# A token-mixing MLP after linear attention on one core: two weight sums of the second product made ahead in device memory, five wide products, and an order written by hand

## The chip, the cores and the metric

The kernel runs on one core of one Trainium2 chip. The metric is the device time of one execution in microseconds (us), the median of several runs. A core has five engines with a queue of instructions each: TensorE (PE, matmuls), VectorE (DVE), ScalarE (ACT), GpSimd (POOL) and SyncE (SP, which here only issues transfers). An engine takes its instructions in order; waits between engines go by semaphores.

## The reference, cut to what matters

```python
x = A_x                                                   # 2048 tokens x 512 channels
h = x + attention(layernorm(x), wqkv, w_phi, wo)          # 32 heads, linear attention with softmax features
g = layernorm(layernorm(h))
u = gelu(einsum("bsd,sf->bdf", g, w1) + b1)               # w1: 2048 x 1792, mixes tokens
y = einsum("bdf,fs->bds", u, w2) + b2                     # w2: 1792 x 2048
out = h + transpose(y)                                    # 2048 x 512
```

All data are float32. The change concerns the last product, with w2, and what is prepared for it.

## The kernel before, in words

Large matmuls are made in three parts. A float32 operand is split into a rounded part "hi" and a remainder "lo" (`split`, lines 55 to 58: ACT copies to hi, another engine subtracts), and hi x hi + hi x lo + lo x hi are accumulated in PSUM.

The program has three stretches. First come the weights of attention, K, V and their sums (to about 121 us of the profile), then the queries, the attention output and the second layer norm, tile by tile (`for it in range(NT + 3)`, line 643, to about 280 us). `fills(it)` puts matmuls of the first MLP product between them. Its weights w1 come by `stream` (line 604): SP loads a block of two row tiles by 256 columns, ACT splits it (L610), `flush` lets DVE make the remainder (L602). `wf` has four buffers of each, and a block serves twelve matmuls.

Second, the rest of the first product (line 751, to about 386 us): seven pairs p of column blocks, each accumulated over 16 row tiles into PSUM `PU`, followed by GELU on ACT (L726). `operands_u(p)` makes the seven right-hand operands of p from its four quarters: for p = 0 and 1 POOL makes the sums (L733 to L736) and ACT and DVE split them into `un`; for the others DVE makes them, into `uf`.

Third, the second product. It is done as seven products of sums instead of eight products of blocks (a Strassen-Winograd scheme), for each pair `sp` of the 16 row blocks of the output (eight pairs) and each p (seven): 56 `STEPS`. Each of the seven products of a step is three matmuls of 256 columns (line 787), accumulated over p into halves of four PSUM banks `bank`; each pair takes the four banks that the pair before did not use. The left-hand operands are sums of four blocks of w2. `stream_w2` (line 767) handles a group of two steps: SP loads 2 x 256 KB into `wraw` (three buffers), DVE makes four sums (L777 to L780), ACT splits 128x1792 elements into `whi` (two buffers, L57), and DVE makes the remainder `wlo` (two buffers, L58). There are 28 groups. After the seventh step of a pair the banks are drained: ACT copies a half bank (L820), DVE does five operations (L821 to L825), and POOL issues two transfers that add the result to `out` in device memory (L827), where h was stored before. The last pair is drained to `hb`, which has h loaded ahead, by ten DVE operations (L836 to L846) and three stores.

In this stretch the order on each engine is chosen by a scheduler of the framework. In parts of the earlier stretches it is written out (`manual_schedule`): there an engine gets its instructions in the order of the program text.

Of the kernel before, what the change touches and what calls it, by code (L numbers as in the profile page):

```python
# [21 lines left out]
NF = F // P  # L22
NG = 8
# [10 lines left out]
def block_kernel(ctx: ExitStack, tc: tile.TileContext, x, xT, wT, phic, wo, w1, b1, w2, b2,  # L34
# [3 lines left out]
    cst = ctx.enter_context(tc.tile_pool(name="cst", bufs=1))  # L38
    big = ctx.enter_context(tc.tile_pool(name="big", bufs=NT + 2))
# [15 lines left out]
    def split(hi, lo, src, lo_engine):  # L55

        nc.scalar.activation(hi, src, AF.Copy)  # L57
        lo_engine.tensor_sub(lo, src, hi)  # L58
# [507 lines left out]
    def s_x(t):  # L566
        HT[t] = ak.tile([P, D], F32, name="h", bufs=4)
        nc.sync.dma_start(HT[t], x[t * P:(t + 1) * P, :])
# [19 lines left out]
    def s_hn(t):  # L588
        hn = ak.tile([P, D], F32, name="hn")
        nc.scalar.activation(hn, HT[t], AF.Identity, scale=r2[:, t:t + 1], bias=VE[t][:, 1:2])  # L590
        HN[t] = big.tile([P, 2, D], F32R, name="hs", tag="big")
        split(HN[t][:, 0], HN[t][:, 1], hn, nc.gpsimd)

    w1v = w1.rearrange("(k p) f -> p k f", p=P)
    w2v = w2.rearrange("(k p) s -> p k s", p=P)
# [8 lines left out]
    def stream(src, k0, n, c0, w):  # L604
# [4 lines left out]
        nc.sync.dma_start(raw, src[:, k0:k0 + n, c0:c0 + w])  # L609
# [4 lines left out]
    PU, WI, LO = {}, {}, []  # L614
# [28 lines left out]
    for it in range(NT + 3):  # L643
# [47 lines left out]
        if it >= 3 and even:  # L691
            s_hn(it - 3)
        for p in range(2):
# [15 lines left out]

    NP = NF // 2  # L710
    HD = D // 2
# [38 lines left out]

    for p in range(NP):
        while FN[p] < NT:
            fill(p, ps_b)
# [10 lines left out]
    GRP = 2  # L764
    AW = {}

    def stream_w2(n):
        steps = STEPS[n:n + GRP]
        raw = ws.tile([P, GRP, 7, P], F32, name="wraw", bufs=3)
        wh_ = ws.tile([P, GRP, 7, P], F32R, name="whi")  # L770
        wl_ = ws.tile([P, GRP, 7, P], F32R, name="wlo")
        for i, (sp, p) in enumerate(steps):
            nc.sync.dma_start(raw[:, i, 0:4].rearrange("p (k i) s -> p k (i s)", k=2),
                              w2v[:, 2 * p:2 * p + 2, sp * 2 * P:(sp + 1) * 2 * P])
            AW[sp, p] = wh_[:, i], wl_[:, i]
        with tc.issue_after(LO[-18]):
            nc.vector.tensor_add(raw[:, :, 4], raw[:, :, 0], raw[:, :, 2])  # L777
            nc.vector.tensor_sub(raw[:, :, 0], raw[:, :, 1], raw[:, :, 0])
            nc.vector.tensor_sub(raw[:, :, 5], raw[:, :, 4], raw[:, :, 1])
            nc.vector.tensor_sub(raw[:, :, 6], raw[:, :, 3], raw[:, :, 5])  # L780
        split(wh_, wl_, raw, nc.vector)


    PROD = ((1, 1, 0, 0, True), (2, 6, 2, 1, True), (3, 3, 3, 1, True), (4, 4, 2, 0, False), (0, 0, 1, 0, True),
            (5, 5, 0, 1, False), (6, 2, 3, 0, False))

    def product(o, a, b, start, stop):
        for i, (x, y) in enumerate(((0, 0), (0, 1), (1, 0))):
            nc.tensor.matmul(o, a[x], b[:, y], start=start and i == 0, stop=stop and i == 2, skip_group_check=True)  # L789

    def products(sp, ps, order):
        for a, b, bk, half, opens in order:
            for p in ps:
                wh_, wl_ = AW[sp, p]
                product(bank[bk][:, half], (wh_[:, a], wl_[:, a]), UB[p, b], p == 0 and opens, p == NP - 1)
# [3 lines left out]

    for n, (sp, p) in enumerate(STEPS):  # L800
        t = 2 * sp
        last = t + 2 == NT
        if n % GRP == 0:
            stream_w2(n)
        if p == 0:
            pools = [ps_f, ps_f, ps_q, ps_q] if sp % 2 else [ps_b] * 4
            bank = [pool.tile([P, 2, HD], F32, name="py", tag="pu") for pool in pools]
        if p < NP - 1 - last:
            products(sp, [p], PROD)
# [3 lines left out]
        by_bank = sorted(PROD, key=lambda m: m[2:4])  # L813
# [3 lines left out]
        if not last:  # L817
            products(sp, [p], by_bank)
            ot = uo.tile([P, 2, 2, HD], F32, name="ot", bufs=1)
            nc.scalar.activation(e[:, 1], bank[0][:, 0], AF.Copy)  # L820
            nc.vector.tensor_add(u2, bank[0][:, 1], e[:, 1])  # L821
            nc.vector.tensor_add(u3, bank[1][:, 0], u2)
            nc.vector.tensor_add(e[:, 0], bank[2][:, 0], u2)
            for i, add in enumerate((u3.unsqueeze(1).to_broadcast([P, 2, HD]), e)):
                nc.vector.scalar_tensor_tensor(ot[:, i], bank[2 + i], b2s[:, t + i:t + i + 1], add,  # L825
                                               op0=ALU.add, op1=ALU.add)
                nc.gpsimd.dma_start(out[(t + i) * P:(t + i + 1) * P, :], flat(ot[:, i]), accum_op=ALU.add)  # L827
# [6 lines left out]
        products(sp, [p - 1, p], by_bank)  # L834
        nc.scalar.activation(e[:, 1], bank[0][:, 0], AF.Copy)
        nc.vector.tensor_add(hb[1][:, 1], bank[0][:, 0], hb[1][:, 1])  # L836
        nc.vector.tensor_add(u2, bank[0][:, 1], e[:, 1])
        nc.vector.tensor_add(hb[1][:, 0], u2, hb[1][:, 0])
        nc.vector.tensor_add(u3, bank[1][:, 0], u2)
        nc.vector.tensor_add(hb[0], hb[0], u3.unsqueeze(1).to_broadcast([P, 2, HD]))  # L840
        nc.vector.tensor_add(hb[0][:, 0], bank[2][:, 0], hb[0][:, 0])
        nc.vector.tensor_add(hb[1][:, 0], bank[2][:, 0], hb[1][:, 0])
        nc.vector.tensor_add(hb[0][:, 1], bank[2][:, 1], hb[0][:, 1])
        nc.sync.dma_start(out[t * P:(t + 1) * P, :], flat(hb[0]))
        for k, q in ((0, nc.scalar), (1, nc.sync)):
            nc.vector.tensor_add(hb[1][:, k], bank[3][:, k], hb[1][:, k])  # L846
            q.dma_start(out[(t + 1) * P:NT * P, k * HD:(k + 1) * HD], hb[1][:, k])
# [14 lines left out]

# [32 lines left out]
```

## Time and profile before

| what | us |
|---|---|
| median of 3 runs | 534.54 (534.31 to 534.79) |
| span of the profiled execution | 532.6 |
| PE busy / DVE busy / ACT busy / POOL busy | 520.8 / 384.4 / 271.9 / 234.8 |
| chain that ended last: second product's matmuls | 26% of the span |
| first product's rest, 280 to 386: PE busy | 106.00 |
| second product, 386.0 to 524.2: PE / DVE / ACT busy | 138.20 / 106.83 / 50.02 |

The span is the time from the first to the last instruction of the one execution that was profiled. The page shows busy time by engine, the chain of work that ended last (followed back from the last instruction) and groups of equal instructions; a group's row ends with the idle time of the engine ahead of it and with what ended that. "windows" gives busy time in stretches of the span, "waits" who waited for whom, "timeline" the instructions in order of time. An instruction's reported duration overlaps a little with the start of the next, so the pace of an engine is read from the distance of starts.

### The profile page before, as it was taken

Reading aid. Unit: us, or ns where it says so; the run is one execution under the profiler, and the core shown is the slowest. Engines: PE = TensorE matmul, PEld = TensorE weight load, DVE = VectorE, ACT = ScalarE, POOL = GpSimd, SP = SyncE. Lnnn points to the kernel's source line nnn. Section 1 sums busy time; section 2 is a strip of 40 time slices with the busy share of each in tenths; the row PEclk is TensorE's granted clock in tenths of the full one; section 3 lists DMA queues with packets and bytes.
Section 4 is the critical chain, followed back from the end, with each engine's and each line's share of the span. In section 5 each row is a group of like instructions: output and inputs, shape, how many; then the busy total and the mean of one; then the engine's idle time right before and its main releaser. Section 6 shows DMA issues by size and latency. Waiting matters only on the chain.

```text
span 532.6 us, 9386 instructions
## 1 busy us (share of the span) xinstructions
PE 520.8 (98%) x3616; PEld 448.7 (84%) x3616; DVE 384.4 (72%) x680; ACT 271.9 (51%) x460; POOL 234.8 (44%) x190
## 2 busy tenths in 40 slices
PE   8999999999999989999999999999999999999995
PEld 7888888886877767777788888888899999999995
DVE  6993999877699989875325524835668877887784
ACT  6998844424336776557746423525444243343340
POOL 2589699877889988887325000000001101100110
PEclk9999999999999999999999999999999999999999
DMA  8633310020502233334255333542014556535631
GB/s 309 206 110 118 99 22 21 1 72 9 160 0 79 82 101 116 104 116 136 85 176 159 98 100 98 159 117 82 20 41 107 143 148 153 123 120 136 143 75 46
DMA packets 45486, 55.81 MB, mean 105 GB/s; under 512 B 3969, under 2 KB 33025, under 8 KB 45441
## 3 DMA queue, kind: packets, MB, share of 16 engines
q1 hardware_dynamic: 43136, 51.38, 30.7%
q0 software_dynamic: 2016, 3.67, 5.5%
q8 instruction: 28, 0.46, 0.4%
q10 hardware_dynamic: 288, 0.17, 0.1%
q14 instruction: 18, 0.14, 0.1%
HBM read 46.81 MB, written 8.39 MB: 104 GB/s over the span
## 4 chain that ended last, share of the span: by engine, by line
PE 83%; POOL 9%; DVE 3%; ACT 2%; issue 1%; DVEq 0%; POOLq 0%; ACTq 0%
PE py L789 26%; PE pu L62 11%; PE pu L63 11%; PE pu L64 11%; POOL ez L442 4%; POOL eq L460 3%; PE pv L63 2%; PE pv L64 2%; PE pv L62 2%; PE pk_ps L62 2%; PE pk_ps L63 2%; PE pk_ps L64 2%; POOL hs L58 2%; PE po L62 1%; PE kvp L207 1%; PE po L63 1%
## 5 line engine op out<-in xcount | busy, mean ns | idle before, releaser
L827 POOL DMA_DIRECT2D out<-ot x14 | 12.5, 1001 | 212.2 <-DVE ot L825 212.2
L789 PE MATMUL py<-uf,whi 128*128 128x256 f32 x560 | 96.2, 283 | 0.0
L63 PE MATMUL pu<-hs,whi 128*128 128x512 f32 x224 | 87.6, 391 | 1.8 <-POOL hs L58 1.8
L602 DVE TENSOR_TENSOR wlo<-wraw,whi 128x512 fp32r<-128x512 f32 x56 | 50.3, 903 | 51.8 <-ACT whi L610 50.7
L57 ACT ACTIVATE whi<-wraw 128x1792 fp32r<-128x1792 f32 x28 | 47.7, 1705 | 77.9 <-PE py L789 73.8
L62 PE MATMUL pu<-hs,whi 128*128 128x512 f32 x224 | 87.4, 395 | 0.0
L64 PE MATMUL pu<-hs,wlo 128*128 128x512 f32 x224 | 87.2, 390 | 0.0
L789 PEld LDWEIGHTS py<-uf,whi 128*128 128x128 f32 x560 | 83.3, 192 | 0.0
L789 PE MATMUL py<-uf,wlo 128*128 128x256 f32 x280 | 69.9, 283 | 0.0
L58 DVE TENSOR_TENSOR wlo<-wraw,whi 128x1792 fp32r<-128x1792 f32 x28 | 56.6, 2022 | 15.4 <-ACT whi L57 15.4
L610 ACT ACTIVATE whi<-wraw 128x512 fp32r<-128x512 f32 x56 | 35.0, 627 | 47.0 <-PE pu L63 44.8
L63 PEld LDWEIGHTS pu<-hs,whi 128*128 128x128 f32 x224 | 42.1, 188 | 11.0 <-POOL hs L58 2.8
L62 PEld LDWEIGHTS pu<-hs,whi 128*128 128x128 f32 x224 | 42.0, 188 | 10.9 <-issue 2.5
L64 PEld LDWEIGHTS pu<-hs,wlo 128*128 128x128 f32 x224 | 42.0, 188 | 9.1 <-DVE wlo L602 0.4
L789 PEld LDWEIGHTS py<-uf,wlo 128*128 128x128 f32 x280 | 49.7, 192 | 0.0
L442 POOL TENSOR_TENSOR ez<-eq,zB 128x1024 f32<-128x1024 f32 x16 | 40.9, 2559 | 2.5 <-ACT zB L488 2.5
L789 PE MATMUL py<-un,whi 128*128 128x256 f32 x224 | 38.4, 283 | 0.0
L195 POOL TENSOR_TENSOR pk<-pk,sk 128x1024 f32<-128x1024 f32 x16 | 31.0, 1941 | 9.8 <-DVE sk L194 9.0
L460 POOL TENSOR_TENSOR eq<-eq,w 128x1024 f32<-128x1024 f32 x16 | 32.0, 1997 | 4.0 <-DVE w L457 4.0
L789 PEld LDWEIGHTS py<-un,whi 128*128 128x128 f32 x224 | 33.2, 192 | 0.1
L199 POOL TENSOR_TENSOR zacc<-zacc,pk 128x1024 f32<-128x1024 f32 x13 | 31.3, 2405 | 0.6
L58 POOL TENSOR_TENSOR hs<-hn,hs 128x512 fp32r<-128x512 f32 x16 | 21.4, 1340 | 17.5 <-ACT hs L57 15.6
(165 smaller groups left out, 1176.5 us busy)
## 6 DMA issues: line engine op xcount, KB each, us to landing
wraw<-in_w SPq DMA_DIRECT2D x112, 256.0 KB, 2.9
xraw<-in_xT SPq DMA_DIRECT2D x16, 256.0 KB, 3.1
xh<-in_x SPq DMA_DIRECT2D x16, 256.0 KB, 2.6
h<-in_x SPq DMA_DIRECT2D x16, 256.0 KB, 2.7
out<-h SPq DMA_DIRECT2D x16, 256.0 KB, 3.0
out<-ot POOLq DMA_DIRECT2D x14, 256.0 KB, 4.8
wraw<-in_wT SPq DMA_DIRECT2D x12, 256.0 KB, 5.0
wo<-in_wo SPq DMA_DIRECT2D x4, 256.0 KB, 3.6
```

What stands on the lines that cost most here:

```text
L57: nc.scalar.activation(hi, src, AF.Copy)
L58: lo_engine.tensor_sub(lo, src, hi)
L62: nc.tensor.matmul(o, ah, bh, start=first, stop=False)
L63: nc.tensor.matmul(o, ah, bl, start=False, stop=False)
L64: nc.tensor.matmul(o, al, bh, start=False, stop=last)
L195: nc.gpsimd.tensor_mul(heads(PK[t]), heads(PK[t]), sk.unsqueeze(2).to_broadcast([P, 2 * H, DH]))
L199: nc.gpsimd.tensor_add(zacc, zacc, PK[t])
L442: nc.gpsimd.tensor_mul(EZ[t], EQ[t], zB)
L460: nc.gpsimd.tensor_mul(heads(EQ[t]), heads(EQ[t]), W[t].rearrange("p g c h -> p (g c h)").unsqueeze(2).to_broadcast([P, 2 * H, DH]))
L602: LO.append(nc.vector.tensor_sub(wl_, raw, wh_).ins)
L610: nc.scalar.activation(wh_, raw, AF.Copy)
L789: nc.tensor.matmul(o, a[x], b[:, y], start=start and i == 0, stop=stop and i == 2, skip_group_check=True)
```

## The change

1. **Layout.** The host lays w2 out by groups: `w2[g]` holds four blocks of 128 x 256 (two steps side by side), g = 0 to 27. Only the arrangement changes, no arithmetic is done there.
2. **Sums in device memory.** A scratch tensor `w2s` in device memory gets block 0 of each group twice by plain transfers from SP (`copies_w2`, two groups of both copies in 2 x 256 KB per iteration of the attention loop, iterations 1 to 14), and then blocks 1 and 2 of the group are added to the copies by accumulating transfers from POOL (`adds_w2`, eight of them for four or three groups each, queued after the last POOL operation of the second layer norm). So A+B and A+C of the blocks A, B, C, D come from memory.
3. **A group's preparation.** SP loads the two sums and B, C, D (256 + 384 KB). DVE makes two more sums (L805, L806), ACT splits (L807, `whi` now with three buffers), DVE makes the remainder (L816).
4. **Wide products.** Five of the seven products get a whole bank: one matmul of lhs hi with 512 columns (rhs hi and lo side by side, so hi x hi falls in one half of the bank, hi x lo in the other), and one of lhs lo x rhs hi with 256 columns into the first half. The drain adds the halves. Two products stay as three matmuls of 256, as the last product of the last pair does. A pair takes six banks of eight in turn.
5. **Drain.** Twelve DVE operations of 256 columns instead of five (two of them of 512); fourteen instead of ten for the last pair. The sixth and seventh step of every pair are done together, product by product.
6. **Order.** From the second product on, `manual_schedule` holds for PE, DVE and ACT.
7. The space kept for descriptors of POOL's transfers is 8192 bytes per partition.

Cut to its core:

```diff
+        if 0 < it < 15:
+            with tc.issue_after(HT["ins"]):
+                copies_w2(2 * it - 2, 2 * it)
...
+    def copies_w2(g0, g1):
+        first = w2[g0:g1, 0].rearrange("g p f -> g (p f)")
+        for k in range(2):
+            nc.sync.dma_start(rows(w2s[g0:g1, k].rearrange("g p f -> g (p f)"), 32), rows(first, 32))
+    def adds_w2(g0, g1):
+        nc.gpsimd.dma_start(rows(w2s[g0:g1].rearrange("g k p f -> g (k p f)"), 64),
+                            rows(w2[g0:g1, 1:3].rearrange("g k p f -> g (k p f)"), 64), accum_op=ALU.add)
...
     for p in range(NP):
+        if p < 4:
+            for g in range(7 * p, 7 * p + 7, 4):
+                with tc.issue_after(HN["ins"]):
+                    adds_w2(g, min(g + 4, 7 * p + 7))
         while FN[p] < NT:
             fill(p, ps_b)
...
+    def load_w2(g):
+        RAW[g] = ws.tile([P, 7, GRP * P], F32, name="wraw", bufs=3)
+        nc.sync.dma_start(RAW[g][:, 0:2], w2s[g].rearrange("k p f -> p k f"))
+        nc.sync.dma_start(RAW[g][:, 2:5], w2[g, 1:4].rearrange("k p f -> p k f"))
+    def sums_w2():
+        ...
+        load_w2(g)
+        raw = RAW[g]
+        WH[g] = ws.tile([P, 7, GRP * P], F32R, name="whi", bufs=3)
+        nc.vector.tensor_add(raw[:, 5], raw[:, 1], raw[:, 2])
+        nc.vector.tensor_add(raw[:, 6], raw[:, 4], raw[:, 5])
+        nc.scalar.activation(WH[g], raw, AF.Copy)
+    def lo_w2():
+        ...
+        wl_ = ws.tile([P, 7, GRP * P], F32R, name="wlo", bufs=2)
+        nc.vector.tensor_sub(wl_, RAW[g], WH[g])
...
+    with tc.issue_after(LO[-18]), tc.issue_after(LD[-20]):
+        sums_w2()
+        lo_w2()
+        sums_w2()
...
+        if half is None:
+            nc.tensor.matmul(o, a[0], b, start=start, stop=stop, skip_group_check=True)
+            nc.tensor.matmul(o[:, 0], a[1], b[:, 0], start=False, stop=stop, skip_group_check=True)
+            return
...
+    ctx.enter_context(tc.manual_schedule(engines={ET.PE, ET.DVE, ET.Activation}))
...
+        if n % GRP == 0 and p < NP - 1:
+            lo_w2()
+            sums_w2()
...
+            nc.scalar.activation(e[:, 1], bank[0][:, 0], AF.Copy)
...
+            out_block(0, 0, bank[2][:, 1], u3)
+            out_block(0, 1, bank[3][:, 0], u3, bank[3][:, 1])
+            nc.gpsimd.dma_start(out[t * P:(t + 1) * P, :], flat(ot[:, 0]), accum_op=ALU.add)
+            if n % GRP == 0:
+                lo_w2()
+            out_block(1, 0, bank[4][:, 0], e[:, 0], bank[4][:, 1])
+            out_block(1, 1, bank[5][:, 0], e[:, 1], bank[5][:, 1])
+            nc.gpsimd.dma_start(out[(t + 1) * P:(t + 2) * P, :], flat(ot[:, 1]), accum_op=ALU.add)
+            if n % GRP == 0:
+                sums_w2()
```

More of the change, by code (lines that the diff above doesn't have):

```diff
@@ L763, in block_kernel @@
     STEPS = [(sp, p) for sp in range(NT // 2) for p in range(NP)]
[L764 to L781, printed above, removed]
@@ L802, in block_kernel @@
         last = t + 2 == NT
-        if n % GRP == 0:
-            stream_w2(n)
+        if n % GRP == 0 and p < NP - 1:
+            lo_w2()
+            sums_w2()
         if p == 0:
[L806 to L809, printed above, removed]
+            bank = []
+            for _ in range(6):
+                pool = (ps_f, ps_q, ps_b, ps_b)[n_bank % 8 // 2]
+                bank.append(pool.tile([P, 2, HD], F32, name="py", tag="pu"))
+                n_bank += 1
+        order = LAST if last else PROD
+        if p < NP - 2:
+            products(sp, [p], order)
             continue
```

99 lines of the change are left out of this document (63 added, 36 removed).

## The prediction

> **What bounds the kernel now.** I read the page's busy row and chain first, then the windows, the chain in order of time, and the waits of the last stage.
>
> ```profile
> span 532.6 us, 9386 instructions
> PE 520.8 (98%) x3616; PEld 448.7 (84%) x3616; DVE 384.4 (72%) x680; ACT 271.9 (51%) x460; POOL 234.8 (44%) x190
> ...
> PE 83%; POOL 9%; DVE 3%; ACT 2%; issue 1%; DVEq 0%; POOLq 0%; ACTq 0%
> ```
> ```profile
> 280.00:386.00 106.00, 106.00 (x470) 87.80 (x469) 55.76 (x107) 46.35 (x84) 7.97 (x8) 1.00 0.35 104
> 386.00:524.20 138.20, 138.20 (x1154) 138.20 (x1154) 106.83 (x166) 50.02 (x42) 12.48 (x14) 1.00 0.48 115
> ```
> ```profile
> 277.65 0.91 PE pu L62 x4
> 385.99 138.25 PE py L789 x1152
> 524.26 0.39 ACT e L835
> 524.68 0.42 DVE hb L836
> ...
> 528.48 0.33 DVE hb L846
> ```
>
> TensorE (PE) bounds the kernel, and in the last two stages without a gap: 106.00 busy of 106.00 us in the first MLP product, 138.20 of 138.20 in the second. In a window row the numbers after the length are PE, PEld, DVE, ACT, POOL. The chain gives the pace: 138.25 / 1152 = 120.0 ns for a matmul of 256 columns, and about 0.91 / 4 = 227 ns for one of 512. The second product has 1176 of them: 141.1 us. The granted clock is 1.00. So PE is worth something per instruction, but only as long as VectorE (DVE, 106.83 us in that window) and ScalarE (ACT, 50.02) deliver the split weights in time. How far they are from the path today:
>
> ```profile
> ACT whi L57 <- PE py L789: 73.8, 25, 3.3
> DVE wlo L58 <- ACT whi L57: 14.9, 12, 3.0
> ```
> ACT waits 73.8 us in 25 waits for PE to give a whi buffer back: the split runs one whole group ahead and stands idle, because the sums of the next group were already made while it waited.
>
> **The change, part 1: PE.** Five of the seven products of a step become one matmul of 512 columns and one of 256 instead of three of 256: 227 + 120 = 347 ns instead of 360. A step is then 5 x 347 + 2 x 360 = 2455 ns instead of 2520, a group (two steps) 4.91 us. Over 49 steps, and 7 with four wide products: 49 x 65 + 7 x 52 = 3.5 us. PE alone would need 137.6 us.
>
> **Part 2: the order written out for DVE and ACT.** The sums drop from four to two a group, but the manual order puts them in a closed loop. At each even step the program says: remainder of group g (wlo, after L816), sums of g+1 (L805, L806), split of g+1 on ACT (L807); the remainder of g+1 comes at the next even step, first on DVE. The split needs its sums, the sums stand behind the previous remainder in DVE's queue, and the next remainder needs the split. Nothing in this circle overlaps with itself. Its pieces, from the timeline of before:
>
> ```profile
> 441.04 0.42 DVE L779 TENSOR_TENSOR wraw<-wraw 128x256 f32<-128x256 f32 x1
> 441.37 0.42 DVE L822 TENSOR_TENSOR u<-py,u 128x256 f32<-128x256 f32 x1
> ...
> 441.71 0.41 DVE L823 TENSOR_TENSOR e<-py,u 128x256 f32<-128x256 f32 x1
> ...
> 443.69 2.01 DVE L58 TENSOR_TENSOR wlo<-wraw,whi 128x1792 fp32r<-128x1792 f32 x1
> 445.62 0.42 DVE L777 TENSOR_TENSOR wraw<-wraw 128x256 f32<-128x256 f32 x1
> 446.07 0.42 DVE L778 TENSOR_TENSOR wraw<-wraw 128x256 f32<-128x256 f32 x1
> ...
> 446.43 1.71 ACT L57 ACTIVATE whi<-wraw 128x1792 fp32r<-128x1792 f32 x1 [3.33 <-PE py L789]
> ...
> 448.17 2.03 DVE L58 TENSOR_TENSOR wlo<-wraw,whi 128x1792 fp32r<-128x1792 f32 x1 [0.88 <-ACT whi L57]
> ```
> The remainder gives DVE free after 445.62 - 443.69 = 1.93 us; a sum followed by one that needs it takes 446.07 - 445.62 = 0.45; the second sum ends 0.42 later; ACT takes 1.71; the remainder starts 448.17 - 446.43 - 1.71 = 0.03 after it, and I put 0.05 for the hand-over to ACT. Loop: 1.93 + 0.45 + 0.42 + 0.05 + 1.71 + 0.03 = 4.59 us a group, against 4.91 on PE. That alone would just do.
>
> But the results of each pair of row blocks are drained in the same DVE queue, and ACT's copy of bank 0 stands behind the split of the next group. The drain has twelve DVE instructions of 256 columns (before: five). Six need their predecessor, 0.45 each; six don't, 441.37 - 441.04 = 0.33 each: 4.7 us. ACT's copy puts 0.3 more into the circle:
>
> ```profile
> L820 ACT ACTIVATE e<-py 128x256 f32<-128x256 f32 x7 | 2.7, 385 | 6.0 <-PE py L789 6.0
> ```
> (385 ns, less what overlaps at its ends.) So each of seven drains adds 5.0 us to the circle; where the remainder is put into the middle of the drain (every other pair), the sums still stand behind its last four instructions, so the sum is the same. Two pairs are seven groups: 7 x 4.59 + 2 x 5.0 = 42.1 us on DVE and ACT, and 14 x 2.455 = 34.4 on PE. **The circle is the longer one; PE waits for wlo.** Three whi buffers don't help, because it is the order, not a buffer, that closes it.
>
> Stage: the remainder of group 2 needs the wlo buffer of group 0, 4.9 us in; from there 25 loops to group 27, 25 x 4.59 = 114.8, and 0.3 because the first still goes by PE; 7 x 5.0 = 35.0 of drains; the last remainder 2.1; the last two steps on PE 4.9. Together 162.0 us, against 141.1: **+20.9**. If the hand-overs are 0.08 and 0.05 longer, it is 25 x 0.1 = 2.5 more; if the drain's dependent instructions go at 0.38, 3 less. Range of this term: +18 to +24.
>
> **Part 3: tail.** After the last matmul (its last bank needs one add) DVE's chain is what ends last, now and then. Before, ten adds follow bank 0, from 524.68 to 528.81, 1.7 us after PE's end (385.99 + 141.1 = 527.1). After, bank 0 is ready 4.2 us ahead of the end, and fourteen adds with the same pace end about 2.1 us after it: **+0.4**.
>
> **Part 4: the transfers.** 28 copies of 256 KB, two per iteration, go into SP's queue after the loads of h; 8 accumulating transfers of 1 and 0.75 MB go into POOL's queue, in front of the first operands_u.
>
> ```profile
> q1 hardware_dynamic: 43136, 51.38, 30.7%
> q0 software_dynamic: 2016, 3.67, 5.5%
> ```
> ```profile
> wraw<-in_w SPq DMA_DIRECT2D x112, 256.0 KB, 2.9
> ```
> The copies move 7.3 MB more; at q1's rate (30.7% of 532.6 us for 51.38 MB) that is 23 us of all engines, spread over some 110 us in which the 16 engines are idle two thirds. A w1 block has four buffers of 12 matmuls, 10.9 us, for a landing of 2.9; I cost the copies at nothing, and up to 3 us if a load of h or w1 stands behind two of them. The adds, at q0's rate, are 7.3 / 3.67 x 5.5% x 532.6 = 59 us of all engines, beside a stage whose own share is 0.35 of 106 us: 37 + 59 of 106. Full, but the first w2s block is wanted only some 50 us later. What costs is their issue on POOL:
>
> ```profile
> L827 POOL DMA_DIRECT2D out<-ot x14 | 12.5, 1001 | 212.2 <-DVE ot L825 212.2
> ```
> ```profile
> 273.45 1.30 POOL L58 TENSOR_TENSOR hs<-hn,hs 128x512 fp32r<-128x512 f32 x1 [1.97 <-DMA wraw<-in_w]
> 280.26 0.73 POOL L733 TENSOR_TENSOR tt<-u 128x256 f32<-128x256 f32 x1 [5.51 <-ACT u L726]
> ...
> 289.92 1.68 POOL L736 TENSOR_TENSOR tt<-u,tt 128x256 f32<-128x256 f32 x1
> ```
> ```profile
> 285.16 0.64 ACT L610 ACTIVATE whi<-wraw 128x512 fp32r<-128x512 f32 x1
> ...
> 291.63 0.85 ACT L57 ACTIVATE un<-tt 128x768 fp32r<-128x768 f32 x1 [1.89 <-POOL tt L736]
> ```
> An accumulating transfer of 256 KB in 128 runs occupies POOL 1.0 us. Eight of them cost 8.0 us if the count of transfers sets it, 14.0 if the runs do (256 and 192 instead of 128: 4 x 2.0 + 4 x 1.5), 28 if the bytes do. I take 11, between the first two. POOL is free from 274.75; with the adds it starts operands_u at 274.75 + 11 = 285.8 instead of 280.26, 5.5 late. Behind it in ACT's queue stand un and then w1's splits. The last split ahead of them (285.16) leaves PE some 10.9 us of work, to 296; a little of un's lateness is made up by POOL and ACT closing up. The second un would end at 292.5 + 5.5 = 298.0 and the next split 0.7 later, less some 0.7 closed up: **+2.0** on PE (none at 8, about 5 at 14, about 19 at 28).
>
> The Trainium skill says in "DMA: Bandwidth & Descriptors", section "Anatomy of one DMA", that descriptor generation is small and that many descriptors can be emitted before the incremental cost shows up. By that the issue is 8.0 us, PE loses nothing here and the sum is 2.0 less; no row of this trace has an accumulating transfer of another size.
>
> ACT's order there changes too. In the built order one split of w1 stands behind both GELUs of the pair p = 2 and an uf split, where before three splits stood ahead of them:
>
> ```profile
> 298.31 0.69 ACT L726 ACTIVATE u<-pu,b1s 128x512 f32<-128x512 f32 x1 [1.63 <-PE pu L64]
> 298.90 0.62 ACT L610 ACTIVATE whi<-wraw 128x512 fp32r<-128x512 f32 x1
> 299.42 0.68 ACT L726 ACTIVATE u<-pu,b1s 128x512 f32<-128x512 f32 x1
> ```
> GELU needs PE's last matmul of the pair, and PE's next matmul needs that split: 0.57 + 0.57 + 0.31 + 0.63 and hand-overs of 0.1 = **+2.2** once, which nothing hides.
>
> Sum: 20.9 + 0.4 + 2.0 + 2.2 = +25.5, a span of 558.1. The median stands 534.54 - 532.6 = 1.9 above the profiled span, so 560.0 us.
>
> **Rivals.** *A, faster: PE stays the bound.* If DVE and ACT kept ahead (the splits of two groups in flight, as before), only part 1 and the tail would count: 532.6 - 3.5 + 0.4 + 1.9 = 531.4 us, 533.6 with the ACT order's 2.2. For it speaks that DVE has fewer busy us in sum (28 x 2 sums less, 7 x 7 drain instructions more). Against it: it holds from a loop of (34.4 - 10.0) / 7 = 3.5 us a group, and the remainder and the split alone are 1.93 + 1.71 = 3.64. Chance 0.05, a third of it within 0.2%. By the Trainium skill, "TensorE: Matmul & The Clock Gate", section "Wait — 56ns, not 53.3ns?", a matmul costs its columns at 2.4 GHz and some 2.5 ns, so a wide product would save 2.5 ns and not 13; A would be 2.8 us longer by it. The rows (120.0 and 227 ns) say 13.
>
> *B, much slower: the adds starve w1.* If issue goes by bytes (28 us on POOL) or w1's loads wait behind the adds, the first product loses about 19 us instead of 2: 577 us. The filled engines (0.35 share and 59 us more) speak for it, the 10.9 us of buffered w1 against. Chance 0.10.
>
> *C, the circle is only half closed.* If DVE drains while ACT splits (1.71 us hidden in each drain), the stage is 7 x 1.71 = 12 us shorter: 548 us. ACT's copy behind the split speaks against it in both kinds of pair. Chance 0.08.
>
> Forecast: 0.77. The range 547 to 571 takes in the bounds of the stage (-3, +3), of the issue (-2, +3), of the copies (+3) and C, and leaves out A and most of B. This kernel's measurement tells about 0.2% from no change. Faster 0.04, within 0.2% 0.01, slower 0.95.
>
> **What would show it.** In the profile after: py matmuls of about 137.6 us in all, with some 24 us of idle before them put down to DVE wlo; ACT's split released by DVE wraw instead of PE; DVE wlo released by ACT whi in most of its 28 cases; starts of wlo 4.6 us apart within a pair and about 9.5 us across a drain in every other pair; POOL's eight issues of about 1.4 us between 275 and 290; two gaps of about 2 us on PE near 297 to 305. I am wrong if PE shows no idle in the second product, or if DVE waits for DMA there.

## The result, and the profile after

The changed kernel takes **574.24 us** (572.69 to 575.46), the kernel before 534.48 (534.31 to 534.79) beside it: a ratio of 1.074, 95% interval 1.0718 to 1.0762. The forecast of 560.0 had the direction, and the time lies 3 us above the top of its range.

The profiled execution of the changed kernel, from its page: the span, the busy times, and the shares of PE and of the DMA engines in forty slices.

```profile
span 571.5 us, 8913 instructions
PE 531.5 (93%) x3343; PEld 437.5 (77%) x3343; DVE 384.8 (67%) x677; ACT 271.0 (47%) x460; POOL 240.8 (42%) x198
...
PE   8999999999999899999996899999987987888886
...
DMA  8534200024405555663899775320263653653541
```

PE, 98% busy before, is 93% busy, and its row has two soft places: a digit 6 in the twenty-second slice (300 to 314 us, in the first MLP product), and sevens and eights through the second product. The DMA row has an 8 and two 9s up to the first place (slices 20 to 22, 271 to 314 us). So there are two losses, and the windows give their sizes (length, then PE, PEld, DVE, ACT, POOL busy, granted clock, DMA share, GB/s):

```profile
280.00:398.20 118.20, 109.58 (x472) 88.89 (x471) 51.52 (x93) 48.55 (x85) 9.85 (x12) 0.99 0.65 167
398.20:566.40 168.20, 147.81 (x903) 128.26 (x902) 113.10 (x182) 47.93 (x42) 12.09 (x14) 0.98 0.46 112
307.30:310.60 3.30, 3.30 (x8) 2.62 (x9) 0.60 (x1) 0.00 (x0) 0.00 (x0) 0.50 1.06 225
```

The second product begins at 398.2 instead of 386.0, **12.2 us later**, and lasts 168.2 us instead of before's 141 (its 1176 matmuls at 120.0 ns), **27 longer**; the tail is 0.8 shorter (571.5 - 566.4 = 5.1 against about 5.8). Together 38.6 of the 571.5 - 532.6 = 38.9 us. The last row is one of the stretches of about 3.4 us that follow an idle gap: PE is busy there, but at a granted clock of 0.50.

**The second product.** Who waited for whom from 399 us on:

```profile
ACT whi L807 <- DVE wraw L806: 50.2, 16, 4.7
ACT whi L807 <- issue: 48.7, 6, 8.1
DVE wlo L816 <- ACT whi L807: 32.4, 17, 2.2
...
PE py L832 <- DVE wlo L816: 11.9, 13, 1.4
...
PE py L835 <- DVE e L874: 6.7, 3, 2.4
```

Before, ACT's split waited for PE (73.8 us): it ran ahead. Now it waits for DVE's sums, DVE's remainder waits for ACT's split, and PE waits for the remainder: the closed circle of the forecast. Another 6.7 us PE waits at three drains until DVE has read a bank; there DVE waits for ACT's copy, which stands behind a split (15.1 us in all). (For 48.7 us of ACT's idle time, in six waits, the profile shows no releaser: "issue".) One turn of the circle, in the timelines of DVE and ACT:

```profile
466.80 2.03 DVE L816 TENSOR_TENSOR wlo<-wraw,whi 128x1792 fp32r<-128x1792 f32 x1 [1.90 <-ACT whi L807]
468.74 0.42 DVE L805 TENSOR_TENSOR wraw<-wraw 128x256 f32<-128x256 f32 x1
469.19 0.42 DVE L806 TENSOR_TENSOR wraw<-wraw 128x256 f32<-128x256 f32 x1
471.51 2.03 DVE L816 TENSOR_TENSOR wlo<-wraw,whi 128x1792 fp32r<-128x1792 f32 x1 [1.89 <-ACT whi L807]
```
```profile
469.78 1.70 ACT L807 ACTIVATE whi<-wraw 128x1792 fp32r<-128x1792 f32 x1 [3.01 <-DVE wraw L806]
```

From remainder to remainder it is 471.51 - 466.80 = 4.71 us, in which DVE idles 1.89 and ACT 3.01: each waits while the other works.

**The first product.** ACT splits the blocks of w1 there. Before, from 280 to 386 us, it waited for PE to free a buffer:

```profile
ACT whi L610 <- PE pu L63: 41.1, 23, 2.1
```

Now, from 280 to 399 us and in ACT's timeline:

```profile
ACT whi L614 <- DMA wraw<-in_w: 18.7, 6, 5.2
```
```profile
306.54 0.63 ACT L614 ACTIVATE whi<-wraw 128x512 fp32r<-128x512 f32 x1 [4.20 <-DMA wraw<-in_w]
312.36 0.63 ACT L614 ACTIVATE whi<-wraw 128x512 fp32r<-128x512 f32 x1 [5.18 <-DMA wraw<-in_w]
318.17 0.63 ACT L614 ACTIVATE whi<-wraw 128x512 fp32r<-128x512 f32 x1 [5.18 <-DMA wraw<-in_w]
```

A block comes every 5.8 us, and PE uses one up in 12 matmuls of 227 ns, 2.7 us. The reason is in the transfers: for each queue its packets, MB and share of the 16 engines, and the issues with their time to landing, from 280 to 320 us.

```profile
q0 software_dynamic: 1810, 6.89, 86.2%
q1 hardware_dynamic: 2406, 2.33, 20.0%
...
wraw<-in_w SPq DMA_DIRECT2D x9, 256.0 KB, 17.0
```

The adding transfers (q0) hold the engines, and a load of w1 (q1) takes 17.0 us to land instead of 2.9. The same view from 304 to 316 us, where three blocks run late one behind another:

```profile
q0 software_dynamic: 561, 2.16, 90.1%
q1 hardware_dynamic: 561, 0.54, 16.7%
```

**561 packets of each queue.** By these counts the engines serve the two queues in turn, one packet of each, though one costs much more than the other. By share, 12 us and 16 engines that is 0.901 x 12 x 16 / 561 = 0.308 us for one that adds, 0.167 x 12 x 16 / 561 = 0.057 us for one of a load. A block of w1 is 256 KB in packets of 1 KB, 16 on each engine, so it takes 16 x (0.308 + 0.057) = 5.8 us while adding transfers are queued. That is the distance of the splits above. (The two shares add up to 107%, so the reported times of packets overlap a little. Counted without them: 2.16 MB are 527 packets of 4 KB, and 12 x 16 / 527 = 0.364 us for one of each, again 5.8 us a block.) The Trainium skill has the rule in "DMA: Bandwidth & Descriptors", section "Queues, rings and completion order" (each engine takes turns between queues packet by packet); the trace agrees, and the durations of the packets are the trace's.

### The profile page after: what moved, and what is told of

Its sections match the earlier page's. It is cut to its first block, busy times and chain, and to the rows that moved or that the text cites. A ratio compares the mean times of both kernels' runs of the same rounds, so it can differ in the third digit from the quotient of the medians.

```text
span 571.5 us, 8913 instructions
## 1 busy us (share of the span) xinstructions
PE 531.5 (93%) x3343; PEld 437.5 (77%) x3343; DVE 384.8 (67%) x677; ACT 271.0 (47%) x460; POOL 240.8 (42%) x198
## 5 line engine op out<-in xcount | busy, mean ns | idle before, releaser
L887 POOL DMA_DIRECT2D out<-ot x7 | 6.1, 869 | 232.7 <-DVE ot L883 232.7
L807 ACT ACTIVATE whi<-wraw 128x1792 fp32r<-128x1792 f32 x28 | 47.6, 1701 | 115.1 <-DVE wraw L806 52.0
L67 PE MATMUL pu<-hs,whi 128*128 128x512 f32 x224 | 88.7, 400 | 8.6 <-ACT whi L614 8.6
L68 PE MATMUL pu<-hs,whi 128*128 128x512 f32 x224 | 88.2, 394 | 1.8 <-POOL hs L63 1.8
L816 DVE TENSOR_TENSOR wlo<-wraw,whi 128x1792 fp32r<-128x1792 f32 x28 | 56.6, 2023 | 36.9 <-ACT whi L807 33.9
L831 PE MATMUL py<-uf,whi 128*128 128x512 f32 x195 | 71.1, 398 | 0.0
L832 PE MATMUL py<-uf,wlo 128*128 128x256 f32 x195 | 55.7, 286 | 8.5 <-DVE wlo L816 8.5
L832 PEld LDWEIGHTS py<-uf,wlo 128*128 128x128 f32 x195 | 36.9, 189 | 11.4 <-DVE wlo L816 11.4
L831 PEld LDWEIGHTS py<-uf,whi 128*128 128x128 f32 x195 | 36.8, 189 | 6.9
L831 PE MATMUL py<-un,whi 128*128 128x512 f32 x78 | 31.4, 426 | 1.8 <-DVE ot L881 1.1
L835 PE MATMUL py<-uf,whi 128*128 128x256 f32 x170 | 32.0, 282 | 0.0
```

Of the source, the lines that this page charges most:

```text
L67: nc.tensor.matmul(o, ah, bh, start=first, stop=False)
L68: nc.tensor.matmul(o, ah, bl, start=False, stop=False)
L807: nc.scalar.activation(WH[g], raw, AF.Copy)
L816: nc.vector.tensor_sub(wl_, RAW[g], WH[g])
L831: nc.tensor.matmul(o, a[0], b, start=start, stop=stop, skip_group_check=True)
L832: nc.tensor.matmul(o[:, 0], a[1], b[:, 0], start=False, stop=stop, skip_group_check=True)
```

## The experiments

Each is the changed kernel, or the experiment that is named, with the edit shown. The kernel before was run beside them each time, at 534.41 to 534.85 us.

### e1_swap: the order of sums and remainder

```diff
-            lo_w2()
             sums_w2()
+            lo_w2()
...
             if n % GRP == 0:
+                sums_w2()
                 lo_w2()
             out_block(1, 0, bank[4][:, 0], e[:, 0], bank[4][:, 1])
...
-            if n % GRP == 0:
-                sums_w2()
```

> Only the order of two calls is swapped: at each even step the two sums of group g+2 come ahead of the remainder of g+1 on DVE (in the drain of every other pair both come after the first row block), so ACT's split and DVE's remainder are of different groups and can run side by side. Theory (the circle DVE sums, ACT split, DVE remainder bounds the second product): its 168.5 us fall to about 143, starts of the remainder (wlo) 4.9 us apart like PE's groups, total about 549. Rival 1 (the loads of w2s or their landing bound it): no change, 574. Rival 2 (the wide matmuls are slower than counted): no change beyond 2 us.

Measured: 549.88 us (547.63 to 550.73), ratio 1.0276 (1.025 to 1.0302). The second product takes 146.3 us instead of 168.3; the gaps in the first are as they were. Calling the sums first takes 22 us back, so the circle is the order that was written, not the amount of DVE's work. In the timeline of DVE the sums now stand ahead of the remainder, and while ACT splits what they made, DVE has something to do:

```profile
456.66 0.41 DVE L805 TENSOR_TENSOR wraw<-wraw 128x256 f32<-128x256 f32 x1
457.11 0.42 DVE L806 TENSOR_TENSOR wraw<-wraw 128x256 f32<-128x256 f32 x1
457.45 2.02 DVE L816 TENSOR_TENSOR wlo<-wraw,whi 128x1792 fp32r<-128x1792 f32 x1
```

The remainder starts right behind the sums, with no wait for ACT.

### e2_addsmall: issue without traffic

The eight adding transfers keep their number and their runs, but move 64 of 1024 columns; so 15/16 of the two sums made in memory are left out.

```diff
-        nc.gpsimd.dma_start(rows(w2s[g0:g1]..., 64), rows(w2[g0:g1, 1:3]..., 64), accum_op=ALU.add)
+        nc.gpsimd.dma_start(rows(w2s[g0:g1]..., 64)[:, :, 0:64], rows(w2[g0:g1, 1:3]..., 64)[:, :, 0:64], accum_op=ALU.add)
```

> The eight accumulating transfers keep their count and their runs but move 64 of each 1024 columns, so 15/16 of two sums are left out of the result. Theory (the traffic of the adds starves the loads of w1 between 304 and 319 us): the gaps of 3.1, 1.6 and 3.2 us on PE go, the first product ends 7 to 11 us earlier, total 563 to 567. Rival (the issue of the adds on POOL costs the time): still 574, with the same late operands_u.

Measured: 560.94 us (560.81 to 561.52), ratio 1.0491 (1.0475 to 1.0507). The window of the first product, and POOL's eight issues:

```profile
280.00:385.70 105.70, 105.70 (x468) 87.50 (x467) 52.09 (x93) 47.46 (x85) 9.84 (x11) 1.00 0.45 123
```
```profile
L630 POOL DMA_DIRECT2D w2s<-in_w x8 | 8.4, 2416 | 0.0
```

PE is busy 105.70 of 105.70 us in the first product, and POOL's issue takes 8.4 us just as in the changed kernel. So the 12 us lost there don't come from the issue. The gap that ACT's order makes at 301 us in the changed kernel is gone too; with the smaller transfers the scheduler placed that split between the two GELUs again, so this run takes away both, and the traffic's share is the 12.2 less the 2.1 us of that gap. The second product still takes 168.3 us.

### e3_narrow: three narrow matmuls in place of the wide product

```diff
-            nc.tensor.matmul(o, a[0], b, start=start, stop=stop, skip_group_check=True)
+            nc.tensor.matmul(o[:, 0], a[0], b[:, 0], start=start, stop=stop, skip_group_check=True)
+            nc.tensor.matmul(o[:, 1], a[0], b[:, 1], start=False, stop=stop, skip_group_check=True)
```

> The five wide products go back to three matmuls of 256 columns, with banks, drain and order of the changed kernel. Theory (circle): PE has 27 us idle in the second product and takes the 280 matmuls more out of that; total within 1 us of 574.2. Rival (PE's wide matmuls, seen at 232 to 241 ns, hold the second product): total changes by more than 2 us, up to 3.5 us longer if PE is the bound.

Measured: 574.34 us (573.07 to 574.53), ratio 1.0732 (1.0714 to 1.075), against 574.24 for the changed kernel. Nothing changes: in this kernel what PE does per matmul is worth nothing, because PE isn't the bound.

### e4_spread: later adding transfers

e1_swap, with the adding transfers moved: those for groups 0 to 13 behind the two `operands_u` on POOL, and those for groups 14 to 27 behind the output transfers of the first two row pairs.

```diff
+            for g in range(7 * p, 7 * p + 7, 4):
+                with tc.issue_after(HN["tt"]):
+                    adds_w2(g, min(g + 4, 7 * p + 7))
...
+            if sp < 2:
+                for g in range(7 * sp + 14, 7 * sp + 21, 4):
+                    with tc.issue_after(sent):
+                        adds_w2(g, min(g + 4, 7 * sp + 21))
```

> Swap of e1, and the adds spread: groups 0 to 6 after operands_u(0), 7 to 13 after operands_u(1), the rest on POOL after the output transfers of the first two pairs of the second product. Theory (circle, and traffic of the adds against w1): second product about 143 us, first product 7 to 10 us shorter than in e1, total 536 to 542. Rival (adds hurt wherever they are, now the loads of the second product): the second product has stalls on DMA, total above 546.

Measured: 560.41 us (559.31 to 562.99), ratio 1.0486 (1.0455 to 1.0517). My expectation fell, and the rival that I had named held. The first product is nearly whole again (one gap of 1.82 us at 308.57), but the second takes 166.5 us. Its waits from 388 to 470 us:

```profile
DVE wraw L804 <- DMA wraw<-in_w: 24.3, 2, 12.3
PEld py L831 <- DVE wlo L815: 19.0, 4, 9.8
```

Two bursts of 1.8 MB hold up the loads of w2 by up to 12.3 us, just as the burst in the first product holds up those of w1. So moving a burst elsewhere doesn't cure it; whether spreading does, e9_paced tests.

### e5_pool: the two sums on POOL, nothing in memory

No copies and no adding transfers. POOL makes A+C and A+B from the loaded blocks, and its order is written by hand too; on DVE the order of e8_swap2 (below).

```diff
-        nc.sync.dma_start(RAW[g][:, 0:2], w2s[g].rearrange("k p f -> p k f"))
+        nc.sync.dma_start(raw[:, 0], w2[g, 0])
         nc.sync.dma_start(raw[:, 2:5], w2[g, 1:4].rearrange("k p f -> p k f"))
+        nc.gpsimd.tensor_add(raw[:, 1], raw[:, 0], raw[:, 3])
+        nc.gpsimd.tensor_add(raw[:, 0], raw[:, 0], raw[:, 2])
...
+        if g + 3 < NGR:
+            load_w2(g + 3)
```

> No copies and no adding transfers; the two sums that they made in memory are made by GpSimd, which has nothing but seven pairs of output transfers to issue in the second product, one group of four loads ahead of VectorE's two sums; VectorE's remainders stand ahead of its sums in most steps, behind them where a row pair has just begun draining. If the adding transfers cost the first product 9 us and the circle of VectorE and ScalarE cost the second 27, both are gone: the first product ends as in the kernel before but for the 2.3 us gap of the order of ScalarE, the second takes PE's own time with five wide products, 138 to 142 us instead of 141.0, and the whole is 531 to 538. Rival: GpSimd's sums (0.7 to 1.0 us each at 128x256 by its rows in the first product) make the blocks late, so that the second product stays above 146 us and the whole above 541.

Measured: 542.26 us (542.0 to 543.09), ratio 1.0136 (1.0119 to 1.0153). The first product ends as before, at 385.8 us: without the transfers there is nothing left to explain there. The second takes 149.9 us, so the rival held. Two waits from 395 us to the end, and two groups of DVE:

```profile
POOL wraw L789 <- DMA wraw<-in_w: 101.6, 19, 52.0
ACT whi L804 <- DVE wraw L803: 78.1, 14, 8.2
```
```profile
L803 DVE TENSOR_TENSOR wraw<-wraw 128x256 f32<-128x256 f32 x23 | 13.2, 574 | 0.8
L802 DVE TENSOR_TENSOR wraw<-wraw 128x256 f32<-128x256 f32 x23 | 11.8, 513 | 6.3 <-POOL wraw L789 6.3
```

A block passes through one more engine between its load and the split, with the same three buffers, and a load can start only when the remainder three groups back has been made. DVE's sums also take 574 and 513 ns on average instead of 425 and 420. That is POOL's adds beside them: of the 23 instructions of L803 the 15 that overlap with none take 424 to 427 ns, the 8 that do 843 to 924.

### e6_pool_narrow: e5_pool with narrow products

The edit of e3_narrow in e5_pool.

> As e5_pool, with the five wide products written as three narrow ones again. If PE is the bound there, this costs what a wide product saves, 280 times: 13 ns each by the prediction's working gives +3.6 us against e5_pool, 6 ns by the cadence in the trace of the changed kernel +1.7, 2.5 ns +0.7. If PE is not the bound there, nothing.

Measured: 545.6 us (544.42 to 546.42), ratio 1.0199 (1.018 to 1.0217), 3.3 us above e5_pool. Since e5_pool's PE waits for remainders, that isn't a clean price of the wide product; e10_paced_narrow gives it.

### e7_adds1k: shorter runs

```diff
-    ... rearrange("g k p f -> g (k p f)"), 64) ...
+    ... rearrange("g k p f -> g (k p f)"), 256) ...
```

> The changed kernel with the same bytes added in runs of 1 KB instead of 4 KB. If the long packets are what keeps the loads of w1 waiting (each takes its transfer engine for 333 ns, an ordinary 1 KB packet for about 50), shorter ones let the loads in more often: the first product ends near 387 us instead of 398, and the whole is 562 to 566. If it is the bytes, nothing changes: 573 to 576. If GpSimd's issue follows the number of runs, its eight instructions take over 20 us instead of 8.4 and the traffic is spread over a longer time.

Measured: 577.43 us (577.29 to 577.85), ratio 1.0797 (1.078 to 1.0813). What it should tell is hidden by a new loss. The transfers and the issues, 280 to 320 us, then POOL's and ACT's timelines:

```profile
q0 software_dynamic: 6780, 6.83, 106.5%
...
wraw<-in_w SPq DMA_DIRECT2D x7, 256.0 KB, 7.1
```
```profile
274.76 7.28 POOL L630 DMA_DIRECT2D w2s<-in_w  x4
286.95 1.77 POOL L630 DMA_DIRECT2D w2s<-in_w  x1 [4.91 <-issue]
```
```profile
306.69 1.06 ACT L62 ACTIVATE un<-u 128x1024 fp32r<-128x1024 f32 x1 [19.86 <-POOL u L753]
```

The loads of w1 do land sooner, after 7.1 us instead of 17.0. But an issue now takes 7.28 / 4 = 1.82 us instead of 1.05, the last four are held up, and POOL comes to operands_u only at 304.4 us. ACT's un, ahead of w1's splits in its queue, waits 19.86 us for POOL, and PE has one gap of 13.7 us. This is the first variant of rival B, made by runs and not by bytes. The row of q0 also gives 1.065 x 640 / 6780 = 0.100 us for an adding packet of 1 KB (at most: a share above 100% says that the reported times overlap). By the byte that is dearer than the long ones (0.40 us for 4 KB), but a block of w1 would take only 16 x (0.100 + 0.057) = 2.5 us beside them. e11 and e12 test that with nothing on POOL behind the issue.

### e8_swap2: the order alone, carried through

The transfers of the changed kernel; in the first two steps of a row pair the remainder goes first, then the sums; in the others the sums first; in an even pair's drain both stand behind the first row block.

```diff
-            lo_w2()
-            sums_w2()
+            for make in (lo_w2, sums_w2) if p < 2 else (sums_w2, lo_w2):
+                make()
...
             if n % GRP == 0:
                 lo_w2()
+                sums_w2()
             out_block(1, 0, bank[4][:, 0], e[:, 0], bank[4][:, 1])
...
-            if n % GRP == 0:
-                sums_w2()
```

> The changed kernel with its transfers as they are, and the order of e5_pool on VectorE: remainders ahead of sums in the first two steps of a row pair, sums ahead of remainders in the others, and in an even pair's drain both behind the first row block. e1_swap took 146.3 us for the second product; if the order alone closes the circle, this takes 140 to 143 and the whole is 543 to 547. If the circle is closed already as far as an order can do it, 549 to 551.

Measured: 546.55 us (545.73 to 546.97), ratio 1.0216 (1.0201 to 1.0231). The window of the second product and two waits of it:

```profile
399.40:540.20 140.80, 140.13 (x904) 126.39 (x903) 112.55 (x180) 47.84 (x42) 12.10 (x14) 1.00 0.54 134
```
```profile
DVE wlo L816 <- ACT whi L807: 8.7, 10, 1.9
...
DVE e L874 <- ACT e L873: 5.3, 7, 1.5
```

PE is busy 140.13 of 140.80 us. DVE's wait for the split falls from 32.4 us to 8.7, and in the drains ACT's copy of bank 0 no longer stands behind a split (15.1 us of waiting in the changed kernel, 5.3 here). DVE's wait for the loads, 18.0 us in e1_swap, is 4.7. The whole 27 us of the second product were the order.

### e9_paced: the transfers spread

e8_swap2, with fourteen adding transfers of two groups instead of eight, each behind a copy of one column of a landed block of w1 on POOL, one block in three.

```diff
+            turn["fill"] += 1
+            if turn["fill"] % 6 == 1 and turn["add"] < 28:
+                with tc.issue_after(HN["ins"]):
+                    k = turn["add"]
+                    seen = nc.gpsimd.tensor_copy(pad[:, k:k + 1], LO_RAW[0][:, 0, 0:1]).ins
+                HN["ins"] = seen
+                with tc.issue_after(seen):
+                    adds_w2(turn["add"], turn["add"] + 2)
+                turn["add"] += 2
```

> The order of e8_swap2, and the adding transfers of the changed kernel cut into fourteen of two groups each (0.52 MB, 128 packets of 4 KB), each held back on GpSimd by a copy of one column of a block of w1 that has landed, one block in three, so that they are spread over the first product instead of issued in one burst. 128 packets at 333 ns over 16 transfer engines are 2.7 us, and one block of w1 is wanted about every 2.8 us, so a load is held up by about one period at most, which the ring of loads covers. By the theory (the burst starves w1, the order opens the circle, nothing else costs) the first product ends at 386 to 388 us as in the kernel before, the second takes 140.7, the tail 5.0, and the whole is 532 to 536. Rival: the adding transfers slow the loads however they are spread; then gaps of 2 to 3 us remain on PE in the first product, and the whole is 539 to 546.

Measured: **533.26 us** (532.38 to 534.71), ratio 0.9971 (0.9961 to 0.9981): faster than the kernel before, by 0.3%. Windows of the two products, and the transfers from 277 to 386 us:

```profile
280.00:386.60 106.60, 106.44 (x470) 87.74 (x469) 53.02 (x95) 47.63 (x85) 22.63 (x30) 1.00 0.75 187
386.60:526.10 139.50, 139.50 (x903) 126.47 (x903) 112.56 (x180) 47.86 (x42) 12.08 (x14) 1.00 0.56 135
```
```profile
q0 software_dynamic: 2016, 7.34, 37.9%
...
wraw<-in_w SPq DMA_DIRECT2D x34, 256.0 KB, 5.0
```

The same 7.34 MB are added, beside the same loads, and PE is idle for 0.16 us of the first product and not at all in the second. A load lands after 5.0 us, which the four buffers cover. The gap that ACT's order makes at 301 us in the changed kernel is gone here too: the scheduler placed that split between the two GELUs. Nothing of the change itself costs time; its orders and its burst did.

### e10_paced_narrow: what a wide product saves

The edit of e3_narrow in e9_paced.

> As e9_paced, with the five wide products as three narrow ones. With PE the bound of the second product there, this shows what a wide product saves, 280 times: +3.6 us at 13 ns each, +1.7 at 6 ns, nothing if PE is not the bound.

Measured: 535.13 us (534.37 to 536.04), ratio 1.0006 (0.9997 to 1.0014), 1.87 us above e9_paced for 273 matmuls more. Here PE is the bound, and a wide product is worth 1.87 / 273 = 6.8 ns (good to 2 or 3 ns, since the runs of each kernel spread over 1.7 to 2.3 us). That is about what e9_paced gains on the kernel before: with narrow products it is level.

### e11_burst4k and e12_burst1k: the length of a packet

e8_swap2, with fourteen adding transfers of two groups each in one burst, on POOL behind the second `operands_u` (about 292 us); e12_burst1k is the same, instruction for instruction, with runs of 1 KB (64 becomes 256 in `adds_w2`, as in e7_adds1k).

```diff
-        if p < 4:
-            for g in range(7 * p, 7 * p + 7, 4):
-                with tc.issue_after(HN["ins"]):
-                    adds_w2(g, min(g + 4, 7 * p + 7))
...
         if p < NEAR:
             operands_u(p)
+            for g in range(0, 28 * p, 2):
+                with tc.issue_after(HN["tt"]):
+                    adds_w2(g, g + 2)
```

> The order of e8_swap2, with fourteen adding transfers of two groups each in one burst behind the second operands_u on GpSimd (about 295 us), so that nothing on GpSimd waits behind their issue. In the changed kernel the adding queue and the loading queue each moved 561 packets between 304 and 316 us: one packet of each in turn, on each of 16 transfer engines. If that is the rule, a block of w1 (256 packets of 1 KB, 16 on each engine) takes 16 x (0.308 + 0.057) = 5.8 us as long as the burst lasts, about 41 us, while PE uses one up in 2.7 us. Seven blocks late by 3.1 us each, less what is buffered (8 to 11 us): 11 to 14 us lost, the whole 542 to 547. If the burst hurts only where POOL's own instructions stand behind it, 532 to 535.

> As e11_burst4k, instruction for instruction, but with the adding transfers in runs of 1 KB. By the rule of one packet each in turn a block of w1 takes 16 x (0.100 + 0.057) = 2.5 us, a little less than PE's 2.7, so that the loads keep pace though the burst now lasts longer, 45 us and more: a loss of 0 to 4 us, the whole 532 to 537. If the bytes or the fullness of the engines decide, and not the length of a packet, it loses as much as e11_burst4k or more: 542 to 550.

Measured: 545.3 us (544.99 to 545.36), ratio 1.0203 (1.0187 to 1.0218) with 4 KB, as expected; 542.01 us (541.15 to 542.93), ratio 1.0148 (1.0131 to 1.0165) with 1 KB, in the rival's range. The traces say more than the times. With 4 KB, the packets from 310 to 322 us and ACT's splits:

```profile
q0 software_dynamic: 588, 2.15, 89.6%
q1 hardware_dynamic: 586, 0.57, 17.3%
```
```profile
322.38 0.63 ACT L614 ACTIVATE whi<-wraw 128x512 fp32r<-128x512 f32 x1 [5.02 <-DMA wraw<-in_w]
328.08 0.63 ACT L614 ACTIVATE whi<-wraw 128x512 fp32r<-128x512 f32 x1 [5.07 <-DMA wraw<-in_w]
```

One packet of each again, and a block every 5.7 us; PE has four gaps, which end at 317.4, 323.1, 328.8 and 334.3 us. With 1 KB, ACT's splits and the packets from 322 to 334 us:

```profile
315.00 0.63 ACT L614 ACTIVATE whi<-wraw 128x512 fp32r<-128x512 f32 x1 [2.09 <-PE pu L68]
...
339.47 0.63 ACT L614 ACTIVATE whi<-wraw 128x512 fp32r<-128x512 f32 x1 [15.69 <-DMA wraw<-in_w]
```
```profile
q0 software_dynamic: 1449, 1.44, 74.3%
q1 hardware_dynamic: 1453, 1.41, 43.7%
```

Until 323 us, with more than 25 us of the burst behind it, ACT waits for PE and not for a load: w1 keeps pace beside full engines, as 2.5 us a block says (q1's 1.41 MB in 12 us make it 2.2). Then there is one wait of 15.7 us and one long gap of PE, 6.3. I had left out that SP's queue holds the first three groups of w2 there (issued at 314 to 321 us), ahead of the next block of w1: 3 x 640 KB, and at q1's 1.41 MB in 12 us they take 16.7 us. So the rule of turns stands, the length of the packets sets the price of a load in a burst, and e12's time missed by what else was in the loads' queue (read from the trace; no run moves those loads).

## Why the prediction was right and wrong, step by step

- **Part 2, the circle: right in mechanism, 6.3 us too small.** 162.0 us were forecast, 168.3 measured; e1_swap and e8_swap2 show the cause. This error alone would have made 566 us and that of the adds alone 570, both inside the range; together they left it. Two terms were mis-sized. The loop is 4.71 us instead of 4.59: from the second sum's start to the split's start the trace has 469.78 - 469.19 = 0.59 us, where I put 0.42 + 0.05. That is 25 x 0.12 = 3.0 us. A drain adds 5.4 us instead of 5.0: I put 4.7 us for its twelve instructions, but from 437.43 us to the next remainder at 442.56 they take 5.1, and ACT's copy adds 0.3. I gave each that needs its predecessor 0.45 us; there they follow after 0.46 to 0.53, those behind a `scalar_tensor_tensor` (475 ns itself instead of 420) after 0.51. The figure 5.4 also comes from the pattern of PE's gaps, which recurs with every two row pairs (437.91, 481.68): (43.8 - 7 x 4.71) / 2 = 5.4. That is 7 x 0.4 = 2.8 us. The 0.5 us left over I can't place.
- **Part 4, the adds: wrong, and this is the step that failed.** I computed 59 us of transfer time for 106 us of a stage that already used 37, called the engines "Full", and still costed the traffic at nothing, because nobody waits for the adds themselves for 50 us. What counted was who else waits on the same engines. The size was off too (by the pages they took 0.115 x 571.5 - 0.055 x 532.6 = 36 us of all engines, not 59), but not the wrong way. The transfers were all issued within 8.4 us, so the load was not spread over 106 us but took 86% of all engines for 40 us, and each packet of a load waited for one that adds (e11_burst4k has the same 1 : 1). Of the 12.2 us lost ahead of the second product ACT's order makes 2.1 and the traffic most of the other 10: from start to start three matmuls of PE lie 3.09, 1.60 and 3.17 us apart at 304 to 319 us instead of 0.23, which is 7.2 us, and behind the first of them a stretch of 3.4 us at half clock costs 1.7. About 1.2 us I can't place. e2_addsmall takes the traffic away and e9_paced spreads it; in both it goes. The last part of rival B ("w1's loads wait behind the adds") was true at about half of the price that I gave it (9 to 10 us instead of 19).
- **Part 4, the issue: 2.0 us forecast, 0 measured.** Eight issues take 8.4 us, so it is their count, the lower end; PE lost nothing to it (e2_addsmall). The section "Anatomy of one DMA" of the Trainium skill's "DMA: Bandwidth & Descriptors" had it so, and the changed kernel's trace agrees; e7_adds1k shows the limit of that reading, since with four times the runs an issue takes 1.82 us and some are held up besides.
- **Part 4, ACT's order: right.** +2.2 forecast; the gap that ends at 301.47 is 2.33 us from start to start, 2.1 more than a matmul's pace, and ACT's timeline has the split behind both GELUs and the uf split.
- **Part 4, the copies: right.** They were costed at nothing; e9_paced has all 28 and is faster than before.
- **Part 1, PE: half right.** A wide product saves 6.8 ns, not 13, so PE alone needs 139.5 us and not 137.6 (e9_paced). I added 227 ns for 512 columns, read in the first product, to 120 for 256, but the pair takes 360 - 6.8 = 353 in the second. In e9_paced's timeline three starts in a row lie at 399.77, 400.01 and 400.12 us, 0.24 us for the wide half and 0.11 for the narrow one: the wide half is the term that was too small. The Trainium skill's "TensorE: Matmul & The Clock Gate", section "Wait — 56ns, not 53.3ns?", gives some 2.5 ns as the fixed cost of a matmul; the measured saving lies between that and my 13. In the changed kernel none of this counts (e3_narrow).
- **Part 3, tail: +0.4 forecast, -0.8 measured.** DVE's last add ends 2.23 us behind the start of PE's last matmul instead of 1.99, so that part went the way of the forecast, and the last store lands as far behind it as before (4.0 and 4.1 us). What is shorter lies behind the store, 1.0 us instead of 1.7, and its cause stays open. The late PE isn't it: in e9_paced, where PE isn't late, the tail is just as short.
- **Rivals.** A was excluded for the order as written, and rightly, but it is what the change does once order and burst are mended: 533.26 us, beside the 531.4 that I gave it. C (548 us, a stage of 150) did not happen in the changed kernel, whose stage is 168.3.

Not forecast at all: after some of PE's gaps (in the changed kernel those that end at 307, 438 and 526 us, of 3.1, 2.4 and 2.7 us, not those that end at 319 and 482, of 3.2 and 2.4) PE runs for some 3.4 us at half clock. So a gap can cost 1.7 us beyond its length. Why some gaps do and others don't stays open.

Left open: why e6_pool_narrow costs 3.3 us against e5_pool, which is more than PE's term.

## What to carry to other kernels

Two engines that hand a block back and forth need work of another block between the two halves: put what the partner waits for (the sums) ahead of what waits for the partner (the remainder), and check it at the drains. When transfers are added, don't ask only when their own result is wanted; ask how long the burst that one queue issues fills the engines, what a load costs while it takes turns with those packets, and compare that with how long the buffered blocks last. Before blaming an operation for a loss, change its place or its pace: here the same bytes and almost the same instructions, in another order and at another pace, make 574 us or 533.

## What the runs showed of the hardware

- Adding transfers from memory to memory take about 0.31 us of a transfer engine for a packet of 4 KB (the changed kernel) and 0.10 for one of 1 KB (e7_adds1k), and a load on another queue gets one packet through for each of them (561 and 561, 588 and 586, 1449 and 1453, in windows of 12 us of the changed kernel, e11_burst4k and e12_burst1k).
- The granted clock falls to 0.50 for about 3.4 us after some of PE's gaps of 2.2 us and more from start to start (3.1 us at 307 in the changed kernel, 2.2 us at 475 in e5_pool), and stays at 1.00 where gaps are under 1 us (e8_swap2's second product).
- An instruction of DVE that sums 128x256 takes 843 to 924 ns instead of 425 in 8 of the 8 cases of L803 where POOL adds beside it; of the other sum, L802, only 4 of 11 such cases are slow (e5_pool).
